# Retention, soft experts and a bilinear layer on one core: when the product of two weights is filled in between the experts, and how its conversions are portioned

## The chip, the cores and the metric

The kernel runs on one core of a Trainium2 chip. The metric is the device time of one execution in microseconds (us); the time before is the median of three runs. A profile of one further execution gives the trace from which all rows come. TensorE is called PE in the rows, its weight loads PEld, VectorE DVE, ScalarE ACT, GpSimd POOL, and SyncE, which issues nearly all transfers, SP.

## What is computed

Attention with a decay (8 batches, 8 heads, 576 tokens, 64 features a head), then a soft mixture of 8 experts, then a bilinear layer:

```python
ret = scale * (q @ k^T) * Dmat          # Dmat: gamma**(i-j) for i >= j, else 0
x = (ret @ v) as 4608 tokens x 512
logits = x @ phi                        # 32 slots: 8 experts x 4
d = softmax over tokens;  slot_input = d.T @ x
slot_out[e] = relu(slot_input[e] @ w1[e]) @ w2[e]      # 512 -> 1024 -> 512
x = (softmax over slots of logits) @ slot_out
a = x @ m1;  b = x @ m2
out = (a * b) @ w3 @ w_out              # 1024 x 1024, then 1024 x 512
```

## The kernel before

All instructions stand in an order written out by hand, engine by engine. Each engine, SyncE's queue of transfers too, runs its own instructions in that order, and waits where one needs a result of another engine.

The kernel has four stages. The first (to about 160 us) runs the attention over 36 units of 128 tokens and gathers the slots' inputs. A short second one finishes the softmax over tokens (`slotm` holds the slots' inputs). The third, with which the change has to do, runs the eight experts on the 32 slots (about 171 to 250 us). The fourth multiplies out the bilinear layer over pairs of slots and then over all tokens in 9 blocks of 512.

**The experts.** An expert's weights are eight loads of 512 KB each (`load_expert`, L583): four for the first layer, four for the second. `emit_l1` (L602, then the activation L607) is the first layer, 32 matmuls; `emit_turned` (L615, VectorE) transposes the hidden row, and `emit_l2` (L622) is the second layer, 16 matmuls accumulated over all experts into one bank. The places that the loads fill are a list, `free`: after `emit_l1` and after `emit_l2` four places each return to it, and `load_expert(8)` issues as many loads as there are places. A load waits in SyncE's queue until the matmuls that read its place before are done, and everything behind it in the queue waits too. 19 of the 64 loads are issued before this stage.

**The product of weights.** Since nothing nonlinear stands between them, w3 and w_out are multiplied beforehand (`emit_Ws`, L564). It is 64 groups (counter `nW`) of three matmuls 128x512: four groups for each of 16 half rows ("pieces") of w3. Three groups run before the stage, 52 in experts 0 to 6, three in expert 7, six after. Eight groups fill one bank, which `evict` (ScalarE L572, VectorE L573) then empties.

**The conversions.** The weights of the bilinear layer come as 64-bit floats (loads L479 into four buffers, `raw`) and are converted on the chip in five steps each: ScalarE L502, VectorE L503, ScalarE L504, VectorE L505, VectorE L497 (`conv_list`); GpSimd then adds a part (L523). A piece of w3 is then split for the matmuls into a high and a low part: a copy on ScalarE (`copy`, L528) and a subtraction on GpSimd (`sub`, L533, counter `nsplit`). `convert(n)` emits n steps; the first step of a piece comes in addition. It begins a piece only if one of three buffers of values is free (`can_conv`, L731), which a subtraction frees, and after a piece's last step it issues the next raw load. There are three places for split pieces: `run_copies` (L536) holds a copy back until the groups that read the place are emitted, and `emit_Ws` returns early unless the piece behind the one at hand is split.

**One step.** Each expert has four steps t = 0 to 3 behind `emit_l1`. A step first emits what is pending (`tick`: subtractions, copies, adds, evictions), at t = 1 the transposition; then loads, groups of the product up to a target, at t = 2 the second layer and its loads; then one or two parts of the softmax over slots (`soft`: VectorE and ScalarE, transposes L409 and L390 on TensorE), then `convert`. When the stage begins, three groups are done and 30 of 40 pieces converted, w3's first six among them.

Of the kernel before, what the change touches and what calls it, by code (L numbers as in the profile page):

```python
# [31 lines left out]
def retention_softmoe_bilinear(  # L32
# [65 lines left out]
    def place(tag, name=None, dt=F32):  # L98
        t = new("place", name or tag, 1024, dt, tag=tag)
        all_places.append((t, tag))  # L100
        return t

    def tag_of(t):
        return next(g for x, g in all_places if x is t)
# [310 lines left out]
    def store_expt(last):  # L415
        for T, n in ((0, 8), (8, 1)):
            for g in range(4):
                for o in (0, 32):
                    i = nc.sync.dma_start(
                        out=bass.AP(expt.tensor, expt.offset + 512 * (64 * T + o) + 128 * g, [[512, 32], [64 * 512, n], [1, 128]]),  # L420
                        in_=L["et"][T // 8][32 * g:32 * g + 32, 0:n],
                    )
                    if T + g + o == 0:
                        after(i, last)
# [56 lines left out]
    def load_pieces():  # L481
        while nl[0] < len(pieces) and nl[0] < done[0] + NRAW:
            load_piece(nl[0])
            nl[0] += 1
# [4 lines left out]
    def conv_list(i):  # L489
        t, p = value(turn[i]), parts[i % 2]  # L490
        w = raws[i % NRAW].rearrange("p (n w) -> p n w", w=2)
        lo, hi = w.bitcast(U32)[:, :, 0], w.bitcast(U32)[:, :, 1]
        tu = t.bitcast(U32)
        v = nc.vector

        def last():
            v.scalar_tensor_tensor(out=tu, in0=hi, scalar=0xC0000000, in1=tu, op0=ALU.bitwise_and, op1=ALU.bitwise_or)  # L497
            done[0] += 1
            adds.append(lambda: add(i))

        return [
            lambda: nc.scalar.activation(out=t, in_=w[:, :, 1], func=ACTF.Abs),  # L502
            lambda: v.tensor_scalar(out=t, in0=t, scalar1=W_MIN, scalar2=W_MAX, op0=ALU.max, op1=ALU.min),  # L503
            lambda: nc.scalar.activation(out=p.bitcast(I32), in_=lo, func=ACTF.Copy, scale=2.0 ** -29),  # L504
            lambda: v.tensor_scalar(out=tu, in0=tu, scalar1=3, scalar2=0x3FFFFFFF, op0=ALU.logical_shift_left, op1=ALU.bitwise_and),  # L505
            last,
        ]

    def run_conv(n):
        for _ in range(min(n, len(conv_ops))):  # L510
            conv_ops.pop(0)()
# [32 lines left out]
    nsplit, nW = [0], [0]  # L544
# [7 lines left out]
    def emit_Ws(n, lag=1):  # L552
        for _ in range(n):
            i, k = divmod(nW[0], 4)
            if i == 16 or nsplit[0] < min(9 + i + lag, 24):
                return
            nW[0] += 1
            ps = bank[(5, 2)[i // 2 % 2]]
            b = block(w3p, i % 3)
            ah, al = (b[:, o + 128 * k:o + 128 * k + 128] for o in (0, 512))  # L560
            k8 = 4 * (i % 2) + k
            bh, bl = (t[:, 512 * k8:512 * k8 + 512] for t in (woh, wol))
            for part, (x, y) in enumerate(((ah, bh), (ah, bl), (al, bh))):
                nc.tensor.matmul(out=ps, lhsT=x, rhs=y, start=(k8 == 0 and part == 0), stop=(k8 == 7 and part == 2))  # L564
            if k8 == 7:
                evicts.append(lambda cb=i // 2, ps=ps: evict(cb, ps))

    def evict(cb, ps):
        t = place(tag_of(wplaces[cb]), f"w{cb}", F32R)
        wh.append(t[:, 0:512])  # L570
        wl.append(t[:, 512:1024])
        nc.scalar.copy(out=wh[cb], in_=ps)  # L572
        nc.vector.tensor_tensor(out=wl[cb], in0=ps, in1=wh[cb], op=ALU.subtract)  # L573
# [4 lines left out]
    def load_expert(n=1):  # L578
        loads = []
        while n and free and len(ew) < 8 * NE:  # L580
            e, j = divmod(len(ew), 8)
            ew.append(free.pop(0))
            loads.append(nc.sync.dma_start(out=ew[-1], in_=(ew1, ew2)[j // 4][e][:, 1024 * (j % 4):1024 * (j % 4) + 1024]))  # L583
            n -= 1
        return loads
# [12 lines left out]
    def emit_l1(e):  # L598
        ps = bank[e % 2]
        for k in range(4):  # L600
            for g in range(4):
                last = nc.tensor.matmul(  # L602
                    out=ps[32 * g:32 * g + 32, 0:256], lhsT=slotm[:, 128 * e + 32 * k:128 * e + 32 * k + 32],
                    rhs=ew[8 * e + k][:, 256 * g:256 * g + 256], start=(k == 0), stop=(k == 3), skip_group_check=True,
                )
        hr = tmp.tile([128, 256], F32, tag="h0", name="hr")
        nc.scalar.activation(out=hr, in_=ps[:, 0:256], func=ACTF.Relu)  # L607
        hr_of[e] = hr
        free.extend(ew[8 * e:8 * e + 4])
        return last  # L610

    def emit_turned(e):
        hr = hr_of[e]
        ht = tmp.tile([128, 256], F32, tag="h1", name="ht")
        nc.vector.transpose(out=ht, in_=hr)  # L615
        ht_of[e] = ht

    def emit_l2(e):
        ht = ht_of[e]
        for cb in range(8):  # L620
            qd = cb % 4
            nc.tensor.matmul(  # L622
                out=bank[4][32 * qd:32 * qd + 32], lhsT=ht[:, 32 * cb:32 * cb + 32], rhs=ew[8 * e + 4 + cb // 2][:, 512 * (cb % 2):512 * (cb % 2) + 512],
                start=(e == 0 and cb < 4), stop=(e == 7 and cb >= 4), skip_group_check=True,
            )
        free.extend(ew[8 * e + 4:8 * e + 8])
# [28 lines left out]
    with tc.manual_schedule():  # L655
# [75 lines left out]
        def can_conv():  # L731
            if nconv[0] == nl[0]:
                return False
            j = turn[nconv[0]]
            return 8 <= j < N3 or nth(j) < nsplit[0] + 3
# [167 lines left out]
        def convert(n):  # L903
            while n:
                if not conv_ops:
                    if not can_conv():
                        return
                    conv_ops.extend(conv_list(nconv[0]))
                    nconv[0] += 1
                    run_conv(1)  # L910
                run_conv(1)
                n -= 1
                if adds:
                    load_pieces()

        def tick():
            run(subs)
            run_copies()
            run(adds)
            run(evicts)  # L920
# [4 lines left out]
        def soft():  # L925
            T, step = divmod(nsoft[0], 2)
            if T < NT:
                nsoft[0] += 1
                if step == 0:
                    emit_csoft(T)  # L930
                else:
                    emit_expt(T)
                    if T + 1 < NT:
                        emit_turn(T + 1)
# [3 lines left out]
        for e in range(NE):  # L938
            load_expert(8)
            last = emit_l1(e)  # L940
            if e == NE - 1:
                store_expt(last)
            if e == 0:

                free[:] = [t for t in free if not any(t is x for x in ring)]
                second = tag_of(free.pop(0))
                etp = [place("ew0", "et0"), place(second, "et1")]
                L["et"] = [t.rearrange("p (t n) -> p t n", n=128) for t in etp]
                L["soft"] = [etp[1][:, o:o + 128].rearrange("p (g s) -> p g s", g=4) for o in (512, 640)]
            for t in range(4):  # L950
                tick()
                if t == 1:
                    emit_turned(e)
                load_expert(8)
                emit_Ws(max(0, min(55, 4 + (4 * e + t + 1) * 52 // 28) - nW[0]))
                if e == NE - 1 and t == 1:
                    emit_Ws(3, 0)
                if t == 2:
                    emit_l2(e)
                    if len(wplaces) < 8:  # L960
                        wplaces.append(free.pop(0))
                    load_expert(8)
                while e < NE - 1 and nsoft[0] <= (4 * e + t) * 18 // 28:
                    soft()
                convert(2 + t % 2)
        emit_Ws(1, 0)
        so = acc
        nc.scalar.copy(out=so[:, 0:256], in_=bank[4][:, 0:256])
# [245 lines left out]
```

## Time and profile before

| | us |
|---|---|
| median of 3 runs | 395.93 |
| lowest and highest run | 394.4, 396.1 |
| the profiled execution | 397.17 |
| its span, first to last instruction | 395.4 |
| busy in the span: PE / DVE / ACT / POOL | 377.4 / 254.5 / 198.8 / 172.5 |
| DMA: 108.75 MB, mean | 275 GB/s |

The span is shorter than the execution's own time by what lies around it. [...] The DMA rate and the idle time differ from stage to stage, so both are read by stretches of time.

### The profile page before, as it was taken

To read this page: it belongs to the slowest core of one execution; us is meant where nothing else is said; L and a number is where in the kernel's file an instruction comes from. 1 tells how busy PE (TensorE), PEld (TensorE's weight loads), DVE (VectorE), ACT (ScalarE), POOL (GpSimd) and SP (SyncE) were. 2 spreads that over 40 slices of the span, in tenths; PEclk is the share of its full clock that TensorE was granted. 3 is DMA by queue.
4 is the path that set the end of the run, shared out by engine and by line. 5 is a ranking of instruction groups with operands and counts; after the bars stand their busy time and mean duration, and the time that the engine had idled before them with its cause. 6 is when DMAs were issued, how large, how long until landed. Compare 5 with 4: busy or idle time off the path is not lost.

```text
span 395.4 us, 10962 instructions
## 1 busy us (share of the span) xinstructions
PE 377.4 (95%) x4447; PEld 284.3 (72%) x4447; DVE 254.5 (64%) x432; ACT 198.8 (50%) x424; POOL 172.5 (44%) x158
## 2 busy tenths in 40 slices
PE   6999998999998999899999998999999999999995
PEld 3889786878887886566555553578687777788774
DVE  3458999899887988545776552299766443555410
ACT  2347695788676785414544521235444353444332
POOL 2732765675554554113554431037634434553420
PEclk9999999999999999999999999999999999999999
DMA  7999999799889999997999999692269979999543
GB/s 236 333 330 322 308 352 321 246 385 389 277 278 324 337 319 346 336 409 264 390 400 409 410 408 381 140 219 51 61 127 209 230 190 246 236 218 211 155 98 98
DMA packets 48211, 108.75 MB, mean 275 GB/s; under 512 B 7584, under 2 KB 10016, under 8 KB 48160
## 3 DMA queue, kind: packets, MB, share of 16 engines
q1 hardware_dynamic: 47008, 107.85, 85.3%
q8 instruction: 35, 0.57, 0.6%
q10 hardware_dynamic: 1152, 0.20, 0.3%
q14 instruction: 16, 0.13, 0.1%
HBM read 97.41 MB, written 10.62 MB: 273 GB/s over the span
## 4 chain that ended last, share of the span: by engine, by line
PE 72%; DMA 13%; DVE 11%; ACT 1%; issue 1%; SPq 0%; ACTq 0%; DVEq 0%
PE bank L1130 9%; PE bank L1132 8%; PE bank L1131 8%; PE scores L253 7%; PE output L282 7%; PE bank L564 7%; DMA v<-in_ew 5%; PE output L316 4%; PE state L296 3%; DMA q<-in_ew 3%; DMA st<-in_ew 3%; PE bank L622 2%; PE bank L602 2%; PE pair L215 2%; DMA v<-in_v 2%; PE bank L1121 2%
## 5 line engine op out<-in xcount | busy, mean ns | idle before, releaser
L646 POOL TENSOR_TENSOR cc<-mw_sb,cc 128x512 fp32r<-128x512 f32 x36 | 46.0, 1298 | 56.9 <-ACT cc L645 55.6
L564 PE MATMUL bank<-wop,w3p 128*128 128x512 f32 x192 | 50.9, 407 | 0.0
L523 POOL TENSOR_TENSOR vals<-vals,msb 128x512 int32<-128x512 int32 x24 | 30.8, 1285 | 42.7 <-DVE vals L497 36.8
L263 DVE TENSOR_TENSOR pm<-scores,msb 128x1024 f32<-128x1024 f32 x31 | 37.8, 1220 | 14.6 <-PE scores L253 14.3
L564 PEld LDWEIGHTS bank<-wop,w3p 128*128 128x128 f32 x192 | 34.1, 188 | 15.0 <-issue 8.7
L645 ACT CAST cc<-mw_sb 128x512 fp32r<-128x512 f32 x36 | 22.2, 616 | 43.6 <-DVE mw_sb L644 34.8
L1130 PE MATMUL bank<-w3p,cc 128*128 128x512 f32 x108 | 43.1, 399 | 0.0
L1132 PE MATMUL bank<-w3p,cc 128*128 128x512 f32 x108 | 42.1, 390 | 0.0
L1131 PE MATMUL bank<-w3p,cc 128*128 128x512 f32 x108 | 42.1, 390 | 0.0
L253 PE MATMUL scores<-q,kt 64*128 64x128 f32 x496 | 37.3, 290 | 1.2 <-issue 1.2
L644 DVE TENSOR_TENSOR mw_sb<-lga,raw 128x512 f32<-128x512 f32 x32 | 29.3, 954 | 12.3 <-POOL cc L646 12.1
L282 PE MATMUL output<-pm,v 128*64 128x128 f32 x512 | 35.6, 279 | 1.7 <-issue 1.7
L533 POOL TENSOR_TENSOR w3p<-vals,w3p 128x512 fp32r<-128x512 f32 x16 | 21.1, 1317 | 35.0 <-ACT w3p L528 32.3
L523 POOL TENSOR_TENSOR mw_sb<-mw_sb,msb 128x512 int32<-128x512 int32 x16 | 20.4, 1275 | 31.6 <-DVE mw_sb L497 18.5
L253 PEld LDWEIGHTS scores<-q,kt 64*128 64x128 f32 x496 | 31.1, 192 | 4.2 <-issue 2.4
L1134 ACT ACTIVATE mw_sb<-bank,rz 128x512 f32<-128x512 f32 x36 | 24.7, 685 | 18.7 <-PE bank L1132 9.6
L282 PEld LDWEIGHTS output<-pm,v 128*64 128x64 f32 x512 | 27.5, 136 | 7.0 <-issue 5.8
L220 ACT COPY kt<-pair 128x512 f32<-128x512 f32 x26 | 15.2, 586 | 27.6 <-PE pair L219 27.6
L504 ACT ACTIVATE msb<-raw 128x512 int32<-128x512 uint32 x40 | 27.9, 697 | 0.0
L192 POOL TENSOR_TENSOR k<-kr,msb 128x512 f32<-128x512 f32 (+1 forms) x30 | 25.8, 883 | 3.9 <-PE one L205 2.8
L1130 PEld LDWEIGHTS bank<-w3p,cc 128*128 128x128 f32 x108 | 20.3, 188 | 7.1 <-issue 2.9
L1132 PEld LDWEIGHTS bank<-w3p,cc 128*128 128x128 f32 x108 | 20.3, 188 | 4.4
(226 smaller groups left out, 770.9 us busy)
## 6 DMA issues: line engine op xcount, KB each, us to landing
q<-in_q SPq DMA_DIRECT2D x20, 512.0 KB, 6.4
raw<-expt SPq DMA_DIRECT2D x36, 256.0 KB, 4.3
kr<-in_v SPq DMA_DIRECT2D x16, 512.0 KB, 6.1
v<-in_v SPq DMA_DIRECT2D x16, 512.0 KB, 6.5
raw<-in_m SPq DMA_DIRECT2D x16, 512.0 KB, 6.0
raw<-in_w SPq DMA_DIRECT2D x16, 512.0 KB, 6.7
out_x<-mw_sb SPq DMA_DIRECT2D x64, 128.0 KB, 2.4
q<-in_ew SPq DMA_DIRECT2D x14, 512.0 KB, 10.1
```

What stands on the lines that cost most here:

```text
L192: (nc.vector if first else nc.gpsimd).tensor_tensor(out=Ks[:, :, 0:m, h], in0=K[:, 1 - h, :, 0:m], in1=ktab(c, h)[:, 0:m].unsqueeze(1).uns ...
L253: last = nc.tensor.matmul(out=ps[:, p], lhsT=ktb[u % 2][a, p], rhs=Q[a, :, x, p], start=True, stop=True)
L263: nc.vector.tensor_tensor(out=p_places[u % 2].rearrange("p (g t) -> p g t", g=8), in0=(pair if u == 1 else scores).rearrange("p (g t) -> p ...
L282: last = nc.tensor.matmul(out=xt_view(p)[side(p, h)], lhsT=v_tile(u)[:, 1 - h, x, p], rhs=p_main(u)[:, h, p], start=(block_of(u) == 0 and ...
L504: lambda: nc.scalar.activation(out=p.bitcast(I32), in_=lo, func=ACTF.Copy, scale=2.0 ** -29),
L523: nc.gpsimd.tensor_tensor(out=ti, in0=ti, in1=parts[i % 2].bitcast(I32), op=ALU.add)
L564: nc.tensor.matmul(out=ps, lhsT=x, rhs=y, start=(k8 == 0 and part == 0), stop=(k8 == 7 and part == 2))
L644: eng.tensor_tensor(out=e, in0=x, in1=y[:, m], op=ALU.mult)
L646: nc.gpsimd.tensor_tensor(out=cl[m], in0=e, in1=ch[m], op=ALU.subtract)
L1130: nc.tensor.matmul(out=ob, lhsT=ch[m][:, sl], rhs=gh[m], start=False, stop=False)
L1131: nc.tensor.matmul(out=ob, lhsT=ch[m][:, sl], rhs=gl[m], start=False, stop=False)
L1132: nc.tensor.matmul(out=ob, lhsT=cl[m][:, sl], rhs=gh[m], start=False, stop=(m == 3))
```

## The change

Two lines of a step differ. The target for the groups of w3 times w_out was one line over experts 0 to 6; it now rises by one group in each of the first two steps of experts 0 and 1 and, from expert 2 on, linearly to the same 55 at the end of expert 6. And `convert` is called with 3 in every step instead of 2 and 3 in turn.

```diff
@@ -952,7 +952,8 @@
                 if t == 1:
                     emit_turned(e)
                 load_expert(8)
-                emit_Ws(max(0, min(55, 4 + (4 * e + t + 1) * 52 // 28) - nW[0]))
+                step = 4 * e + t + 1
+                emit_Ws(max(0, (min(5, 3 + step), min(7, 1 + step), min(55, 7 + (step - 8) * 48 // 20))[min(e, 2)] - nW[0]))
                 if e == NE - 1 and t == 1:
                     emit_Ws(3, 0)
                 if t == 2:
@@ -962,7 +963,7 @@
                     load_expert(8)
                 while e < NE - 1 and nsoft[0] <= (4 * e + t) * 18 // 28:
                     soft()
-                convert(2 + t % 2)
+                convert(3)
         emit_Ws(1, 0)
         so = acc
         nc.scalar.copy(out=so[:, 0:256], in_=bank[4][:, 0:256])
```

## Rows read from the trace of the kernel before

**Rows 1.** The page: GB/s moved in 40 equal slices of 9.9 us.

```profile
GB/s 236 333 330 322 308 352 321 246 385 389 277 278 324 337 319 346 336 409 264 390 400 409 410 408 381 140 219 51 61 127 209 230 190 246 236 218 211 155 98 98
```

**Rows 2.** Windows: stretch, length, busy by engine, granted clock, DMA share, GB/s.

```profile
core 0: us, PE busy (x) PEld busy (x) DVE busy (x) ACT busy (x) POOL busy (x), PEclk, DMA share, GB/s
171.28:219.41 48.13, 48.13 (x368) 28.57 (x367) 30.43 (x71) 21.62 (x48) 22.18 (x17) 1.00 0.96 374
174.00:177.00 3.00, 3.00 (x15) 2.45 (x14) 1.88 (x5) 0.54 (x1) 1.28 (x1) 1.00 1.03 414
177.00:192.00 15.00, 15.00 (x130) 8.03 (x128) 8.16 (x19) 7.50 (x16) 6.52 (x5) 1.00 0.82 297
192.00:240.00 48.00, 46.38 (x339) 26.95 (x332) 30.33 (x72) 19.93 (x44) 22.31 (x17) 1.00 1.03 408
240.00:249.50 9.50, 7.97 (x61) 2.80 (x59) 1.14 (x2) 1.24 (x3) 0.00 (x0) 1.00 1.00 332
...
185.00:190.00 5.00, 5.00 (x31) 2.72 (x30) 3.74 (x9) 3.71 (x8) 2.58 (x3) 1.00 0.87 303
```

**Rows 3.** The chain that ended last, 173 to 250 us: start, length, what.

```profile
173.21 4.34 PE bank L564 x18
177.56 1.85 PE bank L622 x16
...
181.18 1.86 PE bank L602 x32
...
187.64 1.85 PE bank L622 x16
...
190.40 1.86 PE bank L602 x32
...
238.56 9.84 DMA v<-in_ew
...
248.45 1.05 PE bank L622 x4
```

**Rows 4.** Timeline of SyncE's queue: start, length of the issue, line, tile and source.

```profile
172.84 0.33 SPq L583 DMA_DIRECT2D k<-in_ew  x1
...
178.62 0.33 SPq L583 DMA_DIRECT2D q<-in_ew  x1
...
184.11 0.33 SPq L479 DMA_DIRECT2D raw<-in_w  x1
...
185.96 0.50 SPq L583 DMA_DIRECT2D q<-in_ew  x1
```

**Rows 5.** Expert loads, all instructions of line L583: from issue to landing.

```profile
DMA to landing us min/median/max: 4.0/10.2/11.0
```

**Rows 6.** Timelines of ScalarE and VectorE, 173 to 184 us (idle time before in brackets).

```profile
173.28 0.38 ACT L607 ACTIVATE hr<-bank 128x256 f32<-128x256 f32 x1 [6.08 <-PE bank L602]
...
173.92 0.62 ACT L528 CAST w3p<-vals 128x512 fp32r<-128x512 f32 x1
179.71 0.27 ACT L410 COPY et<-bank 128x128 f32<-128x128 f32 x1 [5.17 <-PE bank L409]
179.87 0.66 ACT L502 ACTIVATE vals<-raw 128x512 f32<-128x512 f32 x1
...
181.50 0.59 ACT L572 CAST w<-bank 128x512 fp32r<-128x512 f32 x1
...
173.70 0.45 DVE L615 STREAM_TRANSPOSE ht<-hr 128x256 f32<-128x256 f32 x1 [0.98 <-ACT hr L607]
...
180.57 0.43 DVE L503 TENSOR_SCALAR vals<-vals 128x512 f32<-128x512 f32 x1 [4.59 <-ACT vals L502]
...
183.35 0.69 DVE L497 SCALAR_TENSOR_TENSOR vals<-raw,vals 128x512 uint32<-128x512 uint32 x1
```

**Rows 7.** The page's costliest groups: GpSimd's adds and subtractions (busy, mean ns).

```profile
L523 POOL TENSOR_TENSOR vals<-vals,msb 128x512 int32<-128x512 int32 x24 | 30.8, 1285 | 42.7 <-DVE vals L497 36.8
...
L533 POOL TENSOR_TENSOR w3p<-vals,w3p 128x512 fp32r<-128x512 f32 x16 | 21.1, 1317 | 35.0 <-ACT w3p L528 32.3
```

## Prediction

> **What bounds the kernel now.** I read the page's forty slices of 9.9 us first, for the stretch in which transfers are neither saturated nor finished. From about 170 us (all experts' weights still partly to come) the transfer engines run at 400 to 410 GB/s, with one hole: the slice from 178 to 188 us moved 264 GB/s [rows 1]. Next the windows: 414 GB/s in 174 to 177 us, 297 in 177 to 192, 408 in 192 to 240. TensorE is busy all through the hole, and idles only afterwards: 1.6 us in 192 to 240 and 1.5 us in 240 to 249.5 [rows 2]. Then the chain of waits: it ends the expert phase with the last expert transfer (238.56 + 9.84 us) and four L622 products on it, over at 249.5 [rows 3]. So the end of the phase hangs on how early the last transfer lands, and that on the hole.
>
> Who makes the hole? The queue of SyncE: behind the expert loads at 172.84 and half a microsecond later the next one goes out only at 178.62, because its place is read by expert 0's second layer, L622, which begins at 177.56; the raw load of 184.11 waits for a conversion's last step L497 (183.35 on VectorE), and four expert loads queue behind it until 185.96 [rows 3, 4, 6]. A load of 512 KB (0.524 MB) at 408 GB/s takes 1.285 us, and from issue to landing the expert loads take 10.2 us in the median [rows 2, 5]: eight in flight, so that in the saturated stretch SyncE waits for landings, not for places. TensorE is what delays expert 0: between the end of L602 (173.2) and L622 it runs six products of L564, 4.34 us [rows 3].
>
> **The change, part by part.** Counting emit_Ws targets by hand (t runs over four steps per expert; three products are done before): before, experts 0 to 6 run 8, 7, 8, 7, 8, 7, 7 groups; after, 2, 2, 9, 10, 9, 10, 10. Both reach 55 when expert 7 starts, so nothing is added or removed; 11 groups leave the first two experts for the next five. A group is three matmuls, 4.34 / 6 = 0.72 us.
>
> *The first two experts.* L602 of expert 0 ends at 173.2. Two groups (1.45 us) end at 174.65; the transposed hidden row, L615, is there at 174.15 (173.70 + 0.45) [rows 6], so L622 starts at 174.65 instead of 177.56: 2.9 us earlier. It takes 1.85; the softmax's two transposes take 0.3 (between the end of L622, 179.41, and L602 at 181.18 lie two groups and they); L602 of expert 1 takes 1.86: it ends at 178.7 against 183.04. One group, the hidden row's chain (activation 0.38, two softmax operations, L615: ready about 1.5 us after L602's end; expert 0's took 174.15 - 173.21 = 0.94), the second group beside it, 0.3 of transposes: L622 of expert 1 at about 180.5 against 187.64, done at 182.4. No group stands before L602 of expert 2: it starts at 182.4 against 190.40. TensorE is then 8 us ahead.
>
> *The transfers.* The load of 178.62 becomes one of about 175.8, its two followers 176.5 and 177.2. The raw load comes behind conversion steps that no longer have a piece's copy and the eviction L572 between them (before: L410 at 179.71, L502 at 179.87, L572 at 181.50, L497 done at 184.0, 4.3 us in all; the steps alone, one after another, with the fourth taken like the second, 0.27 + 0.66 + 0.43 + 0.43 + 0.69 = 2.5 [rows 6]): L410 at 176.9, L497 done at 179.4, the raw load then, four expert loads by 181.3. At no time after 172.84 is the queue empty. What the hole costs: 15 us x (1 - 297/414) = 4.2 us [rows 2]. Not all comes back: with five loads out in 185 to 190 us the rate was 303 [rows 2], and from 177 to 181 the changed kernel has four or five out, so 4 us x (1 - 303/414) = 1.1 us may stay. Ends 3.1 and 4.2; four loads in flight are nearer to a full queue than the hole's one or two, and the raw loads 35 to 37 now come behind the expert loads that they preceded, which keeps those early; I take 4.0. The last landing moves from 248.4 to 244.4, its products end at 245.5.
>
> *The postponed groups.* Does TensorE get there too? From 171.28 to 219.41 it was never idle [rows 2] and did five L602, five L622 (18.55 us together) and 38 groups: 29.6 / 38 = 0.78 us a group with everything small. Experts 2 to 6 after: 5 x 3.71 + 48 x 0.78 = 56.0 us, from 182.4 to 238.4. Expert 7: 1.86 + 3 x 0.78 + 1.85 = 6.05: 244.4. That is 1.1 us before the transfers' 245.5. The cover is thin: the gain can't be more than 249.5 - 244.4 = 5.1, and each stall of TensorE beyond 1.1 us comes off it.
>
> *The pieces of w3.* A copy into one of three slots waits for the groups that read the old piece (run_copies), so conversion now stands still in expert 1 (no slot of vals is free: convert returns at once) and resumes in expert 2. Per piece GpSimd has an add of 1.29 and a subtraction of 1.32 us [rows 7]; from expert 2 to 7 there are 12 subtractions and 9 adds, 27 us of 56. Each subtraction is issued at least a step before the first group that reads it. The nearest case is the piece whose first group is the second of expert 4's third step: TensorE reaches it 6 groups after L602 ends, 4.3 us; activation 0.38, copy 0.62 and subtraction 1.32 need 2.3 [rows 6, 7]. Margin 2.0 us: cost nothing, if it holds. Conversion steps are the same in number; what can stand ahead of L615 in one expert, activation, copy, eviction on two engines (0.59, and 0.69 like L497), two steps and itself, is 0.38 + 0.62 + 0.59 + 0.69 + 0.86 + 0.45 = 3.6 us, against at least 7 groups, 5.0 us, between L602 and L622 from expert 2 on.
>
> *The raw loads* (six left) move behind later expert loads on SyncE's queue, the last from before expert 5's third load to behind expert 6's fourth. Each waits for an L497 and holds the loads behind it; eight loads in flight (10 us) cover a wait of some 3 us as that of 180 to 184. Cost nothing.
>
> *Behind the phase* nothing changes: from 249.5 to 395.4 (145.9 us) the code is the same and all of it hangs on the last L622; the stores of the softmax start behind L602 of expert 7, which moves by about the same.
>
> [...]
>
> Sum: 395.4 - 4.0 = 391.4 us of span. The profiled execution took 397.17, 1.24 above the median of 395.93, so the forecast for the median is 395.93 - 4.0 = 391.9.
>
> **Rivals.**
> (a) *The hole is only moved.* The earlier loads run dry before the raw load releases the next five: then 177 to 181 still runs at the hole's pace and what is won is the later half only. Half of 4.2: 2.1 us, 393.8. For it: a thin queue ran at 303 of 414 even with five loads in it. Against: four issues between 175.8 and 179.4, two before them still in flight.
> (b) *TensorE becomes the bound.* 1.1 us of cover; 48 groups in five experts with a wait of 0.1 us each give back 4.8 - 1.1 = 3.7 of the 4.0: 395.6. For it: TensorE idled 3.1 us for data even when it was late. Against: the landings move forward by as much as its demand does.
> (c) *Slower: the pieces arrive late.* Place: GpSimd's line in experts 3 to 6, where an add that waits for VectorE stands ahead of a subtraction. If the subtraction ends after TensorE reaches its piece, that is over 2.0 us later than worked out, each of ten pieces holds TensorE for about one such add, 1.29 us: 244.4 + 12.9 = 257.3 against 249.5, 7.8 slower, 403.7. Against: GpSimd is half idle, and the emission keeps it a step ahead.
> [...]
> (e) *It doesn't do what it says*: emit_Ws returns early where too few pieces are split. By my count every target is met in its own step; a shortfall would fall under (b).
>
> **How the numbers follow.** Forecast 0.62, own range by the bounds 3.1 to 5.1: 390.8 to 392.8. (a) 0.15, (b) with (e) 0.16, (c) 0.05, (d) 0.02. A measurement of this kernel tells about 0.5%, 2.0 us, from no change: below 393.9 is faster. The forecast and some 0.12 of (a) and (b) are: 0.74. Slower: (c), (d): 0.07. Same: 0.19. The range reaches from 390.5 (5.1 won, and 0.3 for the spread of the runs) to (a) with its spread, 394.3.
>
> **What would show it.** Right: no window from 177 to 192 us much under 380 GB/s; L622 of expert 0 at about 174.7, L602 of expert 2 at about 182.4; last expert landing near 244.4; TensorE idle under 2 us before it; granted clock 1.00. Wrong: L564 waiting for GpSimd's L533 (rival c), L602 of experts 4 to 7 waiting for transfers by more than before (b), a hole at 177 to 181 (a), or the last landing early and the stretch behind it longer than 145.9 us, which would mean that I misread what follows.

## The result, and the profile after

The changed kernel takes 392.78 us (median) against 395.64 for the kernel before on the same chip. The ratio is 0.9904, with a 95% interval of 0.9881 to 0.9927: 3.8 us less, between 2.9 and 4.7. The medians, over all executions, lie only 2.9 us apart; the ratio leaves out executions over 1.5% longer than the fastest of their kernel (five of the changed kernel's 21, none of the other's), so its 3.8 us are at the high side, and the profile of less_after, which is of such an execution, is not read below. The forecast was 4.0 us less (391.9). The profiled execution took 393.84 us, its span is 392.1.

The page's line of GB/s over forty slices (9.8 us each now) answers to [rows 1]:

```profile
GB/s 241 335 331 333 301 365 323 252 375 376 291 274 313 305 324 331 325 397 371 410 409 408 410 407 389 153 210 39 82 114 207 232 221 227 235 222 210 158 89 103
```

The slice that had moved 264 GB/s moves 371; its neighbours, 409 and 390 before, move 397 and 410. The windows answer to [rows 2] (columns as there; the first row is the whole stage, from the first L602 to the end of the last L622):

```profile
172.72:246.44 73.72, 73.46 (x568) 42.63 (x567) 44.80 (x99) 29.73 (x66) 30.11 (x23) 1.00 1.02 399
177.00:192.00 15.00, 15.00 (x137) 8.39 (x133) 6.71 (x22) 5.60 (x14) 2.96 (x3) 1.00 1.02 388
192.00:240.00 48.00, 48.00 (x358) 29.61 (x354) 34.61 (x70) 21.96 (x48) 26.24 (x20) 1.00 1.03 409
240.00:249.50 9.50, 9.24 (x71) 4.66 (x67) 1.85 (x4) 1.34 (x3) 0.00 (x0) 1.00 0.86 271
```

From 177 to 192 us 388 GB/s instead of 297; TensorE, which had idled 3.1 us behind the hole, idles 0.3. The rate is not even within the fifteen us; the lowest windows of two us, counted from the start of the stage, are these:

```profile
180.72:182.72 2.00, 2.00 (x16) 1.05 (x18) 1.83 (x9) 0.64 (x3) 1.28 (x1) 1.00 0.90 350
184.72:186.72 2.00, 2.00 (x28) 1.20 (x18) 0.00 (x0) 0.38 (x1) 0.00 (x0) 1.00 1.00 332
```

The chain of waits answers to [rows 3] (start, length, what):

```profile
172.79 1.86 PE bank L602 x32
174.65 1.59 PE bank L564 x6
176.24 1.85 PE bank L622 x16
...
178.46 1.86 PE bank L602 x32
...
182.27 1.85 PE bank L622 x16
184.13 1.73 PE bank L602 x32
...
234.82 1.01 PE bank L622 x6
235.85 9.50 DMA v<-in_ew
...
245.39 1.05 PE bank L622 x4
```

In the kernel before, three loads in a row stand in the middle of this chain:

```profile
201.66 10.18 DMA v<-in_ew
211.90 10.15 DMA st<-in_ew
222.11 10.17 DMA q<-in_ew
```

In the changed kernel they are gone: from 172.79 to 235.83 the chain runs on TensorE alone (L602, L622, L564 and the transposes of the softmax), and only the last load, whose place expert 6's second layer frees at 235.83, is still in it. TensorE and the transfers now end close together; how close is measured below.

The stage begins at 172.72, 1.4 us later than in the profile before, and is over at 246.44: 73.7 us long instead of 78.2. SyncE's queue answers to [rows 4]:

```profile
177.30 0.33 SPq L583 DMA_DIRECT2D q<-in_ew  x1
...
180.97 0.33 SPq L479 DMA_DIRECT2D raw<-in_w  x1
...
182.88 0.54 SPq L583 DMA_DIRECT2D q<-in_ew  x1
```

Counted from the first L602, the load that waited for expert 0's second layer leaves at +4.6 us instead of +7.3, the raw load at +8.3 instead of +12.8, the last of the four behind it at +10.2 instead of +14.7.

**How the runs are compared.** The starts of the stage differ by up to 5 us between profiles of nearly the same code, because the first stage does. The stage itself and the stretch behind it repeat. So each experiment below is read by its stage (first L602 to end of last L622, from the timeline of TensorE), and by its ratio to the kernel before, whose intervals are 0.2 to 0.5% wide on either side. The two profiles of one kernel differ by up to 0.5 us in the stage, and most kernels have only one.

| kernel | stage: from, to, length (us) | behind it | ratio to before, interval |
|---|---|---|---|
| before | 171.28, 249.50, 78.2 | 145.9 | |
| before_again | 170.41, 248.11, 77.7 | 146.0 | |
| changed | 172.72, 246.44, 73.7 | 145.7 | 0.9904, 0.9881 to 0.9927 |
| after_again | 175.53, 249.12, 73.6 | 145.7 | 0.9886, 0.9836 to 0.9936 |
| targets_only | 171.91, 245.89, 74.0 | 145.6 | 0.9896, 0.9847 to 0.9946 |
| conv3_only | 171.57, 248.52, 77.0 | 146.0 | 0.9996, 0.9961 to 1.0031 |
| e0_only | 173.38, 247.58, 74.2 | 145.7 | 0.9919, 0.9884 to 0.9955 |
| l2_first | 174.85, 251.96, 77.1 | 145.6 | 0.9972, 0.9938 to 1.0006 |
| l2_first_raw | 171.83, 247.38, 75.6 | 145.6 | 0.9965, 0.9925 to 1.0004 |
| pad_before | 173.35, 251.44, 78.1 | 146.0 | 1.0004, 0.9971 to 1.0037 |
| pad_after | 170.28, 248.10, 77.8 | 145.6 | 0.9989, 0.9958 to 1.0021 |
| less_after | | | 0.9888, 0.9853 to 0.9924 |
| after_raw | 171.52, 245.23, 73.7 | 145.7 | 0.9873, 0.9832 to 0.9914 |
| thin_raw | 171.01, 244.62, 73.6 | 146.0 | 0.9899, 0.9869 to 0.9929 |

### The profile page after: what moved, and what is told of

It is laid out like the page before. It is cut to its first block, busy times and chain, and to the rows that moved or that the text cites. A ratio compares the mean times of both kernels' runs of the same rounds, so it can differ in the third digit from the quotient of the medians.

```text
span 392.1 us, 10958 instructions
## 1 busy us (share of the span) xinstructions
PE 375.4 (96%) x4447; PEld 284.9 (73%) x4447; DVE 257.4 (66%) x432; ACT 199.0 (51%) x424; POOL 172.6 (44%) x158
## 4 chain that ended last, share of the span: by engine, by line
PE 74%; DVE 14%; DMA 8%; issue 2%; ACT 1%; POOL 1%; ACTq 0%; POOLq 0%; DVEq 0%
PE bank L564 10%; PE bank L1131 9%; PE bank L1133 8%; PE bank L1132 8%; PE output L282 6%; PE scores L253 5%; DMA kr<-in_v 4%; PE output L316 4%; PE bank L622 3%; PE bank L602 3%; PE state L296 3%; DMA v<-in_ew 2%; PE one L356 2%; PE bank L1122 2%; PE pair L215 2%; DVE vals L497 2%
## 5 line engine op out<-in xcount | busy, mean ns | idle before, releaser
L564 PE MATMUL bank<-wop,w3p 128*128 128x512 f32 x192 | 50.0, 404 | 0.0
L564 PEld LDWEIGHTS bank<-wop,w3p 128*128 128x128 f32 x192 | 34.4, 188 | 14.4 <-issue 7.1
L644 DVE TENSOR_TENSOR mw_sb<-lga,raw 128x512 f32<-128x512 f32 x32 | 29.3, 955 | 12.3 <-POOL cc L646 12.1
L282 PE MATMUL output<-pm,v 128*64 128x128 f32 x512 | 36.1, 284 | 1.0 <-issue 1.0
L253 PEld LDWEIGHTS scores<-q,kt 64*128 64x128 f32 x496 | 30.3, 187 | 4.8 <-issue 2.9
L282 PEld LDWEIGHTS output<-pm,v 128*64 128x64 f32 x512 | 28.1, 139 | 6.1 <-issue 4.9
L1131 PEld LDWEIGHTS bank<-w3p,cc 128*128 128x128 f32 x108 | 20.3, 188 | 7.1 <-issue 2.9
L503 DVE TENSOR_SCALAR vals<-vals 128x512 f32<-128x512 f32 x24 | 18.5, 772 | 7.6 <-ACT vals L502 7.6
```

What stands on the lines that cost most here:

```text
L253: last = nc.tensor.matmul(out=ps[:, p], lhsT=ktb[u % 2][a, p], rhs=Q[a, :, x, p], start=True, stop=True)
L282: last = nc.tensor.matmul(out=xt_view(p)[side(p, h)], lhsT=v_tile(u)[:, 1 - h, x, p], rhs=p_main(u)[:, h, p], start=(block_of(u) == 0 and ...
L644: eng.tensor_tensor(out=e, in0=x, in1=y[:, m], op=ALU.mult)
L1131: nc.tensor.matmul(out=ob, lhsT=ch[m][:, sl], rhs=gh[m], start=False, stop=False)
```

## The experiments

The theory: experts 0 and 1 free their places earlier, the expert loads that wait for those places fill the hole, and the last transfer, which ends the stage, lands earlier by what the hole had cost. The rivals: the quicker conversions; the groups as a filling for TensorE's later idle time; TensorE as the new bound.

### Both kernels again

> The kernel before once more, for a second profile. The length of the expert stage, from the first L602 to the end of the last L622 (78.2 us in the first profile), is what the comparisons rest on. Theory (the stage repeats, the stage ahead of it varies): 77 to 78.5 us, the stretch behind it 145.6 to 146.0. Rival (the stage varies by some us by itself): outside 76.5 to 79.

> The changed kernel once more, beside its parts on the same chip. Both theories expect the ratio measured before, 0.990 (3.8 us less), within 0.3%; the profile again with no stretch of 177 to 192 us under 370 GB/s and the last expert landing 4 us earlier, counted from the start of expert 0's first layer.

Stages of 78.2 and 77.7 us before, 73.7 and 73.6 after: the difference is 4.3 on the means, and the stretch behind is 145.6 to 146.0 in every kernel here. After_again's span is 394.8, 2.7 more than the changed kernel's first profile; its stage started 2.8 later. What varies lies ahead of the stage.

### Which half of the change

```diff
-                convert(3)
+                convert(2 + t % 2)
```

> Only the new targets for the groups; conversions in portions of 2 and 3 as before. Theory (the gain is the hole in the transfers that is filled because experts 0 and 1 free their places earlier): all of the gain, 3 to 4.5 us, ratio 0.989 to 0.993, since every target is met here too by a count of the emission. Rival (later groups run right behind their pieces, so that the faster conversions are needed): a millisecond's thousandth or more of waits per piece, TensorE waiting for GpSimd's subtraction in experts 3 to 6, gain under 2 us.

The other half, on the kernel before:

```diff
-                convert(2 + t % 2)
+                convert(3)
```

> Only the conversions in portions of three; the targets are those of before. Theory: nothing (within 0.5 us), the hole stays at 178 us with under 100 GB/s, because convert returns early in most steps: it waits for a free buffer of values. Rival (the raw load at 184 us is what made the hole, and it comes earlier with a quicker conversion): 1 to 2 us gained, the second half of the hole smaller.

The targets alone give the whole gain but for 0.3 us, less than the stage scatters (0.9896, stage 74.0); the portions of three give nothing that the ratio shows (0.9996), and leave the hole. The window of conv3_only:

```profile
177.00:192.00 15.00, 15.00 (x127) 8.21 (x129) 9.29 (x20) 7.54 (x16) 6.70 (x5) 1.00 0.84 281
```

281 GB/s, against 297 before. But its stage is 1.0 us under the mean of the two before, where the theory allowed 0.5 and the rival began at 1; whether that is the conversions or the scatter of the stage one profile doesn't settle.

### Two groups in expert 0 only

```diff
-emit_Ws(max(0, (min(5, 3 + step), min(7, 1 + step), min(55, 7 + (step - 8) * 48 // 20))[min(e, 2)] - nW[0]))
+emit_Ws(max(0, (min(5, 3 + step) if e == 0 else min(55, 5 + (step - 4) * 50 // 24)) - nW[0]))
```

> The changed kernel with two groups in expert 0 only; expert 1 and later take the other 50 evenly (8, 8, 9, 8, 8, 9). Theory (freed places fill the hole): between before and after: expert 0's second layer and expert 1's first layer come 3 and 4.4 us earlier, expert 1's second 3 us earlier; gain 2.5 to 4 us. Rival (expert 1's thin filling is the part that matters): gain under 1.5 us.

Expert 0 is enough for nearly all: stage 74.2, 3.8 less than the mean before, ratio 0.9919. Expert 1's second layer comes only 4 us earlier here than before (+12.1, in the changed kernel +9.5), and that makes half a microsecond, no more than the stage scatters.

### Earlier places without postponing a group

In the kernel before, the second layer of experts 0 and 1 stands one step earlier; the groups that it passes follow it within the same expert.

```diff
-                if t == 1:
+                if t == (0 if e < 2 else 1):
                     emit_turned(e)
                 load_expert(8)
-                emit_Ws(max(0, min(55, 4 + (4 * e + t + 1) * 52 // 28) - nW[0]))
+                if e >= 2 or t != 1:
+                    emit_Ws(max(0, min(55, 4 + (4 * e + t + 1) * 52 // 28) - nW[0]))
...
-                if t == 2:
+                if t == (1 if e < 2 else 2):
                     emit_l2(e)
```

> The kernel before, with as many groups in each expert as before, but in experts 0 and 1 the second layer stands one step earlier, ahead of most of its expert's groups. Nothing is postponed to a later expert. Theory (places freed earlier fill the hole): the load of 178.6 us goes out near 176, the first half of the hole (about 2.3 us of transfers) closes, expert 1's first layer is no earlier, so the second half stays in part: gain 1.5 to 2.5 us, ratio 0.9935 to 0.996. Rival (what counts is that groups leave the first experts and fill TensorE's idle time in experts 4 to 7): nothing, within 0.5 us.

The load went out at +4.6 as expected, but the gain of 1.5 to 2.5 us did not come: 0.9972, stage 77.1, 0.85 less than the mean before. The hole was not closed, it had moved. SyncE's queue of l2_first:

```profile
180.68 0.38 SPq L583 DMA_DIRECT2D v<-in_ew  x1
187.71 0.33 SPq L479 DMA_DIRECT2D raw<-in_w  x1
188.13 0.39 SPq L583 DMA_DIRECT2D k<-in_ew  x1
```

and its two windows from +10 to +14 us (columns as in [rows 2]):

```profile
184.85:186.85 2.00, 2.00 (x33) 1.07 (x29) 1.11 (x2) 1.00 (x3) 1.28 (x1) 1.00 0.59 238
186.85:188.85 2.00, 2.00 (x14) 1.06 (x17) 1.58 (x5) 0.56 (x3) 1.13 (x1) 1.00 0.15 37
```

Three loads earlier are three loads less later on: the next transfer leaves at +12.9 (187.71), as before (+12.8), and the low rate falls into +10 to +14 (238 and 37 GB/s) instead of +6 to +10, where the two windows of the kernel before move 236 and 178. Two things could hold the next one: the raw load's wait for a conversion, or expert 1's first layer, still at +9.9, which frees the places of the four loads behind it. The list of SyncE's waits from 174 to 192 us (total, times, longest) names the first:

```profile
SPq L479 <- DVE vals L497: 6.6, 1, 6.6
```

So in l2_first the raw load was put behind those four:

```diff
+        expert = [0]
...
-                if adds:
+                if adds and expert[0]:
                     load_pieces()
...
             load_expert(8)
+            expert[0] = e
...
                 load_expert(8)
+                if e == 1 and t == 0:
+                    load_pieces()
```

> The kernel with the second layer one step earlier in experts 0 and 1, and beside it the first raw load of the stage moved behind the four expert loads that follow it on SyncE's queue. In that kernel without the move the hole had only shifted by 4 us, to 12 to 14 us after the stage's start, and the raw load went out at +12.9. Theory A (the raw load's wait for the conversion holds the queue): the four loads leave at about +10.5 to +12, the hole becomes 2 us shorter, the stage 75 to 76 us. Theory B (the places of expert 1's first layer, which starts at +9.9, are what is short; the raw load waits in their shadow): the hole stays within 0.7 us of its size, the stage 76.5 to 77.5.

SyncE's queue of this kernel:

```profile
182.40 0.33 SPq L583 DMA_DIRECT2D k<-in_ew  x1
...
184.70 0.33 SPq L479 DMA_DIRECT2D raw<-in_w  x1
```

The same two windows:

```profile
181.83:183.83 2.00, 2.00 (x33) 1.07 (x30) 1.10 (x2) 1.00 (x3) 1.29 (x1) 1.00 0.81 258
183.83:185.83 2.00, 2.00 (x14) 1.07 (x17) 1.60 (x5) 0.56 (x3) 1.11 (x1) 1.00 0.80 248
```

The four leave from +10.6 on (182.40), the two windows move 258 and 248 GB/s, and the stage is 75.6 us, 1.5 less. So the raw load's wait held them, for about 1.5 us of the stage. They now leave when expert 1's first layer frees their places, and the windows are still short of 400; in the changed kernel that layer starts at +5.7, and the stage is 1.9 us shorter still. The interval of the ratio, 0.9965, is too wide to show this by itself. The stage of l2_first_raw is 2.4 us under the mean before without a single group postponed: so more than half of the change's 4.3 can be had from earlier transfers alone, which speaks against the groups as a filling for TensorE's later idle time.

### Is TensorE the new bound?

Twenty-four matmuls more, 5.8 us at the 0.24 of [rows 3] (4.34 us for 18), in the kernel before and in the changed one; then 24 of its own left out of the changed one.

```diff
+            for _ in range(6 if nW[0] - 1 in (24, 32, 40, 48) else 0):
+                nc.tensor.matmul(out=ps, lhsT=ah, rhs=bh, start=True, stop=True, skip_group_check=True)
             for part, (x, y) in enumerate(((ah, bh), (ah, bl), (al, bh))):
```

> The kernel before with 24 matmuls more (six ahead of groups 24, 32, 40 and 48, into a bank that the group then begins anew; 5.8 us of TensorE). Theory (before, the transfers are the bound in this stage and TensorE idles 3.1 us): 2 to 3.5 us slower. If TensorE were the bound: 5.8 us slower.

> The changed kernel with the same 24 matmuls. Theory (after the change TensorE and the transfers end within about 1 us of each other): 4.8 to 5.8 us slower than the changed kernel, thus 1 to 2 us slower than before. If the transfers are still the bound by some us: 2 to 3.5 us slower than the changed kernel.

The stage of the kernel before without and with them:

```profile
170.41:248.11 77.70, 74.94 (x568) 41.87 (x567) 42.45 (x99) 29.91 (x66) 30.13 (x23) 1.00 0.98 377
```

```profile
173.35:251.44 78.09, 78.09 (x592) 46.87 (x591) 41.42 (x99) 29.89 (x66) 30.09 (x23) 1.00 0.96 369
```

and of the changed kernel with them:

```profile
170.28:248.10 77.82, 77.82 (x592) 47.17 (x591) 42.44 (x99) 30.05 (x66) 29.95 (x23) 1.00 0.97 375
```

The matmuls cost a little less than 5.8 us. Expert 7's first layer in the changed kernel and in its padded form:

```profile
239.02 1.07 PE L602 MATMUL bank<-xts,slotm 128*32 128x256 f32 x16
```

```profile
242.02 1.07 PE L604 MATMUL bank<-xts,slotm 128*32 128x256 f32 x16
```

That is +66.3 after the stage's start without them and +71.7 with them: 5.44 us later. Experts 4, 5 and 6 are later by 1.36, 2.72 and 4.08, so each six matmuls cost 1.36 us in full: from the first of them, in expert 3, up to expert 7 TensorE waits for nothing in the changed kernel.

The kernel before takes these 5.4 us of matmuls for nothing: ratio 1.0004, stage 78.1. My expectation of 2 to 3.5 us missed. It went by TensorE's visible idle time of 3.1 us; its busy time grew from 74.9 to 78.1 us only, by 3.2, although 5.4 were added, so the busy time before held over 2 us of standing still. The changed kernel with the same matmuls is 4.2 us longer in the stage (77.8 against 73.65), where 4.8 to 5.8 were expected: it could hide 1.3 of 5.4. TensorE shows no idle time in either padded kernel, so alone it needs at most 78.1 - 5.4 = 72.7 or 77.8 - 5.4 = 72.4 us for the stage.

```diff
             for part, (x, y) in enumerate(((ah, bh), (ah, bl), (al, bh))):
+                if part == 2 and k8 < 7 and 24 <= nW[0] - 1 < 51:
+                    continue
```

> The changed kernel without the third matmul of 24 groups (the low part of w3 times the high part of w_out, groups 24 to 50 but those that end a bank): 5.8 us of TensorE left out. Theory (the transfers end last by a little, TensorE close behind): the last landing hardly moves; gain on the changed kernel 0 to 1 us, TensorE idle 4 to 5 us in experts 4 to 7. Rival (TensorE has become the bound, and with it the places that the loads wait for): gain on the changed kernel 2 us or more.

Without these 24 matmuls the ratio is 0.9888; the changed kernel has 0.9904 and 0.9886. Nothing is gained that these intervals show, where 2 us or more were expected of TensorE as the bound: the transfers still end last, and the padded kernel shows by how much, 1.3 us.

### Can the rest of the hole be had?

The move of the raw load, in the changed kernel; then also one group each in experts 0 and 1:

```diff
-(min(5, 3 + step), min(7, 1 + step), min(55, 7 + (step - 8) * 48 // 20))[min(e, 2)]
+(4, 5, min(55, 5 + (step - 8) * 50 // 20))[min(e, 2)]
```

> The changed kernel with the first raw load of the stage moved behind the four expert loads that follow it (it left at +8.3 us after the stage's start, and the first of them right behind it; expert 1's first layer frees their places from about +6.5). Theory A: the four leave 1.5 us earlier, the rest of the hole (332 to 379 GB/s at +6 to +16) fills, the stage 72.8 to 73.4 us instead of 73.7. Theory B (four transfers in flight move less than eight, whoever is first): 73.4 to 73.9.

> The changed kernel with one group each in experts 0 and 1 (50 in the five experts behind them) and the raw load moved as in the run beside it. TensorE alone needs some 72.1 us for the stage (the two padded kernels less 5.8 us). Theory (the transfers still end last by 1.5 us): the first places come 0.5 to 2 us earlier, the transfers end at +72.2 to +73, stage 72.8 to 73.4 us, 0.3 to 0.9 less than the changed kernel. Rival (TensorE's own waits for the hidden row in the emptied experts eat it): 73.5 to 74.5 us.

Neither expectation of a shorter stage came true: 73.7, as theory B of the first had it, and 73.6, in the range of the second's rival (73.5 to 74.5). In thin_raw the hole is gone (407 GB/s from +4 to +20.7 us, the changed kernel 389), and still the stage is not shorter:

```profile
171.01:244.62 73.61, 72.93 (x568) 42.85 (x567) 43.41 (x99) 30.12 (x66) 29.45 (x23) 1.00 1.02 400
```

Where the gain went can be read from two loads, the first that leaves within the stage and the last. Their issues, and their times from issue to landing (last number), in the changed kernel:

```profile
174.28 0.33 SPq L583 DMA_DIRECT2D k<-in_ew  x1
k<-in_ew SPq DMA_DIRECT2D x1, 512.0 KB, 5.6
235.85 0.33 SPq L583 DMA_DIRECT2D v<-in_ew  x1
v<-in_ew SPq DMA_DIRECT2D x1, 512.0 KB, 9.5
```

and in thin_raw:

```profile
172.58 0.33 SPq L583 DMA_DIRECT2D k<-in_ew  x1
k<-in_ew SPq DMA_DIRECT2D x1, 512.0 KB, 6.3
234.94 0.33 SPq L583 DMA_DIRECT2D v<-in_ew  x1
v<-in_ew SPq DMA_DIRECT2D x1, 512.0 KB, 8.6
```

The last lands at +72.6 and +72.5, the first at +7.2 and +7.9. Fifty transfers lie between them, which at the prediction's 1.285 us each take 64.3: they took 65.5 in the changed kernel, 64.7 in thin_raw and 64.3 in after_again. So the rest of the hole was worth 0.8 us, and thin_raw got it; but when its stage began, its transfers were 0.7 us further behind TensorE, and that ate it. The last load also leaves later than in the changed kernel (+63.9 against +63.1), because expert 6's second layer, which frees its place, has more groups ahead of it; that cost nothing, since it took 8.6 us instead of 9.5 and landed 1.3 to 1.4 us behind the load before it in both. The rival's reason is not what ends the stage either: TensorE idles 0.7 us, and the last four products begin only on the last landing. The ratios, 0.9873 and 0.9899, can't be told from the changed kernel's.

## Why the prediction was right

- **What bounds.** The last expert landing ends the stage in both profiles, and the padded kernel before shows that TensorE had room: borne out.
- **The first two experts.** L622 of expert 0, L602 and L622 of expert 1, L602 of expert 2 were forecast at +3.4, +5.5, +9.2 and +11.1 us after the stage's start; they came at +3.5, +5.7, +9.5 and +11.4 (176.24, 178.46, 182.27 and 184.13 less 172.72).
- **The transfers.** The raw load was forecast at +8.1 and left at +8.3. The forecast took 4.0 us between 3.1 and 4.2; the stage is 4.3 us shorter on the means of two profiles each, the whole execution 2.9 (medians) to 3.8 (ratio). The working set a partly filled queue from 177 to 181 us at 303 GB/s; it is slow, but less so, and later once more. So "no window much under 380" holds for the fifteen us (388) and not for their parts (350 and 332), and of the up to 1.1 us that might stay of the hole the forecast took 0.2, while 1.2 stayed in the first profile (65.5 against 64.3 for the fifty transfers) and none in the second.
- **Rival (a), a hole that only moves,** is not what the change does, but it is real: it is l2_first, and there it is as the rival has it, the raw load that keeps the next loads back. Behind the raw load's wait stands a second condition that I had not seen: the places of the next four loads, which expert 1's first layer frees. The change meets both, because the raw load leaves at +8.3 instead of +12.8 and groups are gone ahead of that layer too.
- **The raw loads "cost nothing".** For the changed kernel that holds (after_raw has the same stage). As a general step it was wrong: in l2_first the raw load's wait for a conversion held four loads back and cost 1.5 us.
- **TensorE's cover.** Forecast 1.1 us in the changed kernel, measured 1.3, partly by luck: TensorE alone was put at +73.1 and needs 72.4, the transfers' end was put at +74.2 and came at +73.7. The 0.78 us per group was too much for the postponed groups, because it counted the small things between the groups, the softmax's transposes among them, by group, and they come by expert. Ten groups more at 0.72 make 29.6 + 7.2 + 18.55 = 55.4 us for experts 2 to 6; the forecast was 56.0, measured are 54.9 (184.13 to 239.02). Rival (b)'s premise, 3.1 us of idle time before, was too small: at least 5.4 us could be hidden.
- **The pieces of w3** never held TensorE up enough to matter (rival c): targets_only, in which conversions come in smaller portions, has the same stage, and in pad_after each six matmuls made the next expert later by all of their 1.36 us, so there was no wait that they could have hidden in.
- **The clock.** The chance (d), 0.02, was for a granted clock that falls where the groups are taken away. No run shows that: the granted clock stayed at 1.00 in all windows of the changed kernel's stage, and in thin_raw's stage as well, in which experts 0 and 1 have one group each and TensorE idles 0.7 us. The first stage of the changed kernel's profile shows 0.50 from 126 to 129 us (last section).
- **convert(3)** was said to return early in most steps; alone it does nothing that the ratio shows.

## What to carry to other kernels

When transfers bound a stage and their buffers are freed by matmuls, look for the first moment at which the queue of transfers runs dry, find which matmul frees the next place, and take filler work away ahead of all the layers that free places until the queue is full again; moving only the first of them moved the hole (l2_first, 37 GB/s from +12 to +14 us). Filler can be given back once the queue is full, here with about eight transfers in flight by the prediction's estimate (10.2 us from issue to landing, 1.285 us each), up to what the matmul engine really needs; measure that by adding work until the stage grows, since its busy time didn't tell (in pad_before 5.4 us of matmuls raised it by 3.2). And a transfer that waits for another engine held everything behind it in its queue (6.6 us and four loads in l2_first): put it behind those whose places are free (1.5 us of the stage in l2_first, nothing in the changed kernel, where its wait was 2.0 us).

## What the runs showed of the hardware that I had not expected

TensorE's busy time was elastic: 24 matmuls that cost 5.4 us in pad_after raised it by 3.2 us in pad_before, and the stage stayed at 78.1 us, against 78.2 and 77.7 without them. And much of the execution-to-execution spread (389.6 to 396.3 us for the changed kernel) comes from ahead of the experts: in the thirteen profiles of the table the stage started between 170.3 and 175.5 us, while the stretch behind it stayed within 145.6 to 146.0. In the chains of waits the profiles differ from the first transfers on: after_again's chain holds a load of 9.9 us, which the kernel before's doesn't have:

```profile
10.29 9.93 DMA q<-in_q
```

What goes with a late start is a lower granted clock of TensorE. In the changed kernel's profile TensorE stood idle for 2.0 us ahead of 125.60, and from 126 to 129 us the granted clock was 0.50; sixteen matmuls of L282 took 1.97 us:

```profile
125.60 0.32 PE L253 MATMUL scores<-q,kt 64*128 64x128 f32 x1 [2.01 <-issue]
126.00:129.00 3.00, 3.00 (x38) 2.88 (x36) 2.73 (x5) 1.92 (x5) 0.04 (x1) 0.50 0.87 318
126.92 1.97 PE L282 MATMUL output<-pm,v 128*64 128x128 f32 x16
```

In the kernel before the idle time at the same place was 1.2 us, the clock stayed at 1.00, and the same matmuls took 1.09:

```profile
125.49 0.27 PE L253 MATMUL scores<-q,kt 64*128 64x128 f32 x1 [1.19 <-issue]
126.28 1.09 PE L282 MATMUL output<-pm,v 128*64 128x128 f32 x16
```

Over the whole span, six of the thirteen profiles have a mean granted clock of 0.994 to 0.996 (changed, after_again, targets_only, e0_only, l2_first, pad_before); their stages start at 171.9 to 175.5 us, those of the other seven, with 0.998 to 1.000, at 170.3 to 171.8. In the stage itself the clock was 1.00 in all thirteen. Why the first transfers vary, and with them TensorE's idle time, was not tried.
